# Reordering the first attention step of a delta-rule attention and two-MoE kernel, and moving the router's set-up into the dense rounds

## The chip, the cores and the metric

The kernel runs on one core of a Trainium2 chip. The time is device microseconds of one execution; the median of three runs before the change is 1247.72 us (1247.0 to 1248.55). The core has five instruction streams, each in order: TensorE (PE, with its weight loads PEld), VectorE (DVE), ScalarE (ACT), GpSimd (POOL) and SyncE (SP), which here issues nearly all DMAs. A stream stops at an instruction whose inputs, or whose output buffer, are not ready, and everything behind it in that stream stops too.

## The reference

Three stages, each feeding the next, over 3072 tokens of width 384:

```python
# 1. delta-rule attention, 32 (batch, head) pairs, 768 steps, width 48
for t in range(S):
    y[:, :, t] = einsum('bhd,bhde->bhe', q[:, :, t], state)
    v_old = einsum('bhde,bhd->bhe', state, kt)
    state += beta_t * einsum('bhd,bhe->bhde', kt, vt - v_old)
# 2. dense MoE, 4 experts, hidden width 1024
for e in range(4):
    out += p[:, e:e+1] * (relu(x @ w1[e]) @ w2[e])
# 3. sparse MoE, 8 experts: cosine router with the normalized expert_emb and tau, each token to its best expert
expert_idx = argmax(xn @ en.T / tau, axis=1)
out[mask] = gate_w[mask, None] * (relu(x[mask] @ w1[e]) @ w2[e])
```

## The kernel before, in words

Attention is done in NS = 12 steps of 64 tokens for all 32 pairs at once (two groups x = 0, 1 of eight pair products each). Every value is kept as a sum of two fp16 halves (hi and lo), so each product is three matmuls, and most tiles are made by an ACT instruction for hi and a DVE or POOL instruction for lo. A step loads K, Q, V, normalizes K, transposes K and Q, forms the Gram matrices (`gram_k`, `gram_q`), inverts a triangular matrix on DVE (`inverse`, the "pivots"), solves for W through Z and Y with the right hand side R (`rest`, `solve_z`, `solve_y`, `solve_w`), writes the new state (`state`, `keep_state`) and the outputs xT (`outputs`, `columns`).

The dense MoE works in 16 rounds per step: round i does `hidden(i+1)` (18 matmuls, L569), then the attention pieces of slot 2i, then `second(i)` (12 matmuls, L591), then the pieces of slot 2i+1. ACT makes H hi (L573) and DVE H lo (L574) between the two. Every fourth `second` ends an expert, and its two sums in PSUM are added into the tiles acc0 and acc1: for the first expert by ACT (L599), otherwise by DVE (L601). PSUM holds two such sums, so the next expert's first `second` waits for that.

All order is written by hand: tables of slots (`SLOTS`, `FIRST`, `SECOND`) say when each piece of a step is emitted. The first step (`FIRST`) has nothing to run beside; its slots from -5 to 31 are emitted ahead of the first round. The pieces of step s >= 1 go into the rounds of step s-1.

Beside this the kernel has to prepare things in the same streams:
- The dense weights: 32 halves of 384 KB (`load_w`) are loaded by SP, each split (`split_w`, L552, L556, L557) by two ACT instructions and one of POOL. Twelve are split in the first step and twenty in the rounds (slots 0 to 22).
- The router's set-up: `setup_a` (constants, and the DMAs of expert_emb into the buffer of acc0 and of tau), `setup_b` (casts, a 3-wide index table, norm of expert_emb, split into `eh`; DVE with two trips to ACT), `setup_c` (PE turns `eh`, ACT copies it to `en`; POOL makes an index image in the buffer of acc0 and zeros in the buffer of acc1, and these go out by DMA to `ids` and `xb`).

The last point matters for buffers: acc0 and acc1 have one buffer each (`bufs=1`), and `setup_c` borrows them:

```python
t = ap.tile([128, 384], F32, name="acc0")[0:96, 0:256]
...
z = ap.tile([128, 384], F32, name="acc1")[0:64]
nc.gpsimd.memset(z, 0.0)
...
nc.sync.dma_start(out=rows[:, :, lo:hi], in_=z...)
```

SP issues its DMAs in program order. Eight are in flight: each waits for the DMA eight places earlier. In the first 75 us they are: K, Q, V of step 0 and beta, eight weight halves, K of step 1, fourteen halves, Q of step 1, ten halves, the probabilities p, V of step 1; then the DMA transposes KTB<-KB of step 1 (L207), which wait for K's split into KB (L163, L164).

Of the kernel before, what the change touches and what calls it, by code (L numbers as in the profile page):

```python
# [8 lines left out]
F32 = mybir.dt.float32  # L9
# [22 lines left out]
class Attention:  # L32
# [3 lines left out]
    def __init__(self, ctx, tc, q, k, v, beta, ident, pp, xt_pool):  # L36
# [41 lines left out]
        self.t0 = self.cp.tile([128, 16, 32], F16, name="t0")  # L78
        li = self.li = self.cp.tile([128, 2], I32, name="li")
        nc.gpsimd.iota(li[:, 0:1], pattern=[[0, 1]], base=0, channel_multiplier=1)  # L80
        ti = self.ti = self.wk.tile([128, 16, 32], I32, name="ti", tag="wa")
        nc.gpsimd.iota(ti, pattern=[[-2, 16], [1, 32]], base=0, channel_multiplier=0)
        self.TB = zeroed("TB", [128, 16, 2, 128])
        self.WB = [zeroed(f"WB{x}", [128, 2, 8 * 96 + 32]) for x in range(2)]
        self.SB = [zeroed(f"SB{x}", [128, 2, 8 * 96 + 32]) for x in range(2)]

# [414 lines left out]
class Dense:  # L501
# [114 lines left out]
class Sparse:  # L616
# [648 lines left out]
```

## Time and profile before

| | |
|---|---|
| median of 3 runs | 1247.72 us |
| the profiled execution: its time | 1246.16 us |
| its span in the trace | 1244.4 us |
| PE busy | 1141.7 us (92%) |
| DVE, ACT, POOL busy | 770.1, 627.6, 382.8 us |
| first matmul of the dense rounds (L569) | at 74.07 us |
| first `second` of the rounds (L591) | at 83.75 us |

The span is the time from the first to the last recorded instruction; 1.8 us of the execution lie around it. A row of the timeline gives start, duration, engine, line, operation, output<-input with partitions x elements, and in brackets the idle time of that engine in front of it with what ended it. A buffer that is borrowed has its name by the allocation (acc for the router's scratch). Durations of several instructions (x2, x4) run from the first start to the last end.

### The profile page before, as it was taken

The numbers are of one execution on the slowest core, as the hardware profiler recorded it, in microseconds if no ns is written. First come the engines' busy times: TensorE is split into PE (matmuls) and PEld (weight loads), VectorE is DVE, ScalarE is ACT, GpSimd is POOL, SyncE is SP. The second block draws the span as 40 slices with busy tenths as digits, with TensorE's granted clock in tenths as the row PEclk, the third lists the DMA queues.
The fourth block names the chain that finished last, engine by engine and source line by source line (L and its number), as shares of the span: only waits on it lengthen the run. The fifth ranks groups of instructions, "written<-read, shape, count | busy, mean of one in ns | idle before, by whom it ended". The sixth has DMA issues, their size and how long they took to land. (4 is left out here: it accounts for less than half of the span.)

```text
span 1244.4 us, 34015 instructions
## 1 busy us (share of the span) xinstructions
PE 1141.7 (92%) x13738; PEld 892.0 (72%) x13738; DVE 770.1 (62%) x2811; ACT 627.6 (50%) x1163; POOL 382.8 (31%) x356
## 2 busy tenths in 40 slices
PE   3078899999999999999999999999999999999997
PEld 3066676777777777777777776777777777878886
DVE  7847558777587776877768767687684434212221
ACT  5758655555555555656556565565653142222222
POOL 7637422332323223233233332333321113222221
PEclk9579899999999999999999999999999999999999
DMA  8980144555725555254563555634631094967950
GB/s 177 231 147 17 27 90 120 116 88 138 107 86 108 92 148 104 77 121 79 150 110 93 120 118 136 122 95 115 110 102 29 20 346 96 355 176 242 319 157 29
DMA packets 246162, 159.17 MB, mean 128 GB/s; under 512 B 195231, under 2 KB 229356, under 8 KB 246000
## 3 DMA queue, kind: packets, MB, share of 16 engines
q1 hardware_dynamic: 241600, 147.26, 51.4%
q0 software_dynamic: 4400, 9.68, 2.5%
q8 instruction: 110, 1.80, 0.7%
q14 instruction: 52, 0.43, 0.2%
HBM read 142.53 MB, written 35.80 MB: 143 GB/s over the span
## 5 line engine op out<-in xcount | busy, mean ns | idle before, releaser
L591 PE MATMUL po<-W,H 128*128 128x384 f16 x2304 | 410.9, 328 | 25.0 <-DVE acc L601 11.4
L569 PE MATMUL ph<-xT,W 128*128 128x256 f16 x3456 | 409.8, 274 | 1.5 <-ACT xT L106 1.5
L569 PEld LDWEIGHTS <-W 128*128 128x128 f16 x3456 | 332.1, 98 | 49.2 <-issue 1.8
L591 PEld LDWEIGHTS <-H 128*128 128x128 f16 x2304 | 220.0, 98 | 166.0 <-DVE H L574 16.6
L574 DVE SCALAR_TENSOR_TENSOR H<-ph,H 128x512 f16<-128x512 f32 x192 | 132.0, 688 | 204.1 <-ACT H L573 203.6
L573 ACT ACTIVATE H<-ph 128x512 f16<-128x512 f32 x192 | 113.9, 593 | 143.5 <-PE ph L569 142.0
L755 POOL TENSOR_TENSOR wso<-wst,wso 128x768 f16<-128x768 f32 x64 | 105.7, 1651 | 260.9 <-ACT wst L754 253.0
L1024 DVE SCALAR_TENSOR_TENSOR H<-ph,H 128x512 f16<-128x512 f32 x54 | 37.2, 690 | 154.5 <-ACT H L1023 154.5
L1019 PE MATMUL ph<-xt,slot 128*128 128x128 f16 x1944 | 114.7, 221 | 2.0 <-DMA xt<-g 2.0
L1019 PEld LDWEIGHTS <-slot 128*128 128x128 f16 x1944 | 112.3, 99 | 5.7 <-issue 2.4
L304 DVE TENSOR_TENSOR tt<-tt,pr 128x60 f32<-128x60 f32 (+34 forms) x660 | 111.0, 210 | 0.7
L1036 PE MATMUL po<-slot,H 128*128 128x384 f16 x648 | 110.1, 326 | 0.6 <-DVE H L1024 0.6
L300 DVE TENSOR_TENSOR pr<-tt,KQ 128x60 f32<-128x60 f32 (+34 forms) x660 | 109.0, 203 | 0.8
L1036 PEld LDWEIGHTS <-H 128*128 128x128 f16 x648 | 62.1, 98 | 39.1 <-DVE H L1024 1.0
L1041 POOL DMA_INDIRECT out_dram<-ob,idx x27 | 27.4, 1014 | 170.7 <-ACT ob L1040 80.7
L753 ACT ACTIVATE wso<-wst 128x768 f16<-128x768 f32 x64 | 53.3, 833 | 43.7 <-issue 25.5
L1023 ACT ACTIVATE H<-ph 128x512 f16<-128x512 f32 x54 | 32.2, 597 | 80.2 <-PE ph L1019 77.3
L329 PEld LDWEIGHTS <-TB 128*128 128x128 f16 x1152 | 34.6, 98 | 44.4 <-POOL W L557 24.2
L557 POOL TENSOR_TENSOR W<-W,W 128x768 f16<-128x768 f32 x30 | 50.8, 1705 | 42.8 <-ACT W L556 25.5
L263 POOL TENSOR_TENSOR AO<-G,AO 32x256 f16<-32x256 f32 x48 | 31.7, 660 | 97.9 <-ACT AO L262 95.9
L840 POOL DMA_INDIRECT ids<-idt,si x24 | 25.1, 1045 | 118.8 <-DMA ids<-idt,si 65.4
L1040 ACT ACTIVATE ob<-po,sm 128x384 f32<-128x384 f32 x27 | 15.7, 580 | 82.1 <-PE po L1036 82.0
(253 smaller groups left out, 1447.0 us busy)
## 6 DMA issues: line engine op xcount, KB each, us to landing
slot<-wimg SPq DMA_DIRECT2D x108, 768.0 KB
wst<-in_moe_w_dram SPq DMA_DIRECT2D x65, 384.0 KB
wimg<-wso SPq DMA_DIRECT2D x64, 384.0 KB
W<-in_moe_w_dram SPq DMA_DIRECT2D x15, 384.0 KB
xb<-xr SPq DMA_DIRECT2D x48, 98.0 KB
Kr<-in_k_dram SPq DMA_DIRECT2D x24, 192.0 KB
Qr<-in_q_dram SPq DMA_DIRECT2D x24, 192.0 KB
Vr<-in_v_dram SPq DMA_DIRECT2D x24, 192.0 KB
```

Source lines behind the costliest of these rows:

```text
L300: nc.vector.tensor_tensor(out=p, in0=t[:, :, j:j + 1].to_broadcast([128, m, j]), in1=AT[:, j, 0:j].unsqueeze(1).to_broadcast([128, m, j]), ...
L304: nc.vector.tensor_tensor(out=t, in0=t, in1=p, op=ALU.subtract)
L557: low.tensor_tensor(out=lo, in0=t, in1=hi, op=ALU.subtract)
L569: nc.tensor.matmul(ph[:, i], w1[:, a, k, 128 * i:128 * i + 128], xT[:, b, k], start=(n == 0), stop=(n == 8))
L573: nc.scalar.activation(out=H[:, 0], in_=ph, func=AF.Relu)
L574: nc.vector.scalar_tensor_tensor(out=H[:, 1], in0=ph, scalar=0.0, in1=H[:, 0], op0=ALU.max, op1=ALU.subtract)
L591: nc.tensor.matmul(po[t], H[:, a, i, 128 * t:128 * t + 128], w2[:, b, i], start=(f == 0 and i == 0 and n == 0), stop=(f == 3 and i == 1 an ...
L753: self.nc.scalar.activation(out=o[:, 0], in_=t, func=AF.Copy, scale=scale)
L755: self.nc.gpsimd.tensor_tensor(out=o[:, 1], in0=t, in1=o[:, 0], op=ALU.subtract)
L1019: nc.tensor.matmul(ph[:, i], w[:, a, k, 128 * (i % 2):128 * (i % 2) + 128], xt[:, 3 * b + k], start=(m == 0), stop=(m == 8))
L1024: nc.vector.scalar_tensor_tensor(out=H[:, 1], in0=ph, scalar=0.0, in1=H[:, 0], op0=ALU.max, op1=ALU.subtract)
L1036: nc.tensor.matmul(po, H[:, a, i], w[:, b, i % 2], start=(q == 0 and i == 0 and m == 0), stop=(q == 1 and i == 3 and m == 2))
```

## The change

It concerns the first step, the router's set-up and the splits of the dense weights.
- In `FIRST`: `rest` (R) goes from slots 19, 21 to -1, `gram_q` from 2 to 1, `z`, `y`, `w` from 23, 24, 26 to 20, 22, 24, `out` from 28 to 25 (now ahead of `state` at 27), the K norm of step 1 to slots 8, 20, 25.
- `align` is a DVE copy while `low` is DVE; `low` is POOL from slot 4 to 27, DVE before and behind (K's split for step 1, at slot 28, goes to DVE), and POOL in the rounds.
- The memsets of TB, WB and SB on POOL come behind `setup_a`, which moves ahead of the first step; `setup_columns` moves there too.
- Ten weight halves are split in the first step and 22 in the rounds, slots 0 to 24, each by itself.
- `setup_b` moves from slot 20 of the first step to slot 3 of the rounds, `setup_c` from slot 1 to slot 6.

```diff
+FIRST = dict(SLOTS, split_k=(-5, -5), split_q=-3, turn_k=(-1, -1), turn_q=0, rest=(-1, -1), gram_k=(1, 1),
+             gram_q=(1, 1), align=3, to_lanes=4, split_g=(4, 4), split_p=(4, 4), expand_s=None, init=5,
+             pivots=(1, 3, 3, 2, 3, 2, 3, 2, 3, 2, 3, 3, 1), from_lanes=18, split_t=18, z=20, y=22, w=24, out=25,
+             state=27, keep=27, load_k=2, load_q=18, load_v=22, norm=(8, 20, 25))
...
+    def zero_later(self):
+        for t in self.later:
+            self.nc.gpsimd.memset(t, 0.0)
...
+        if self.low is self.nc.vector:
+            self.nc.vector.tensor_copy(self.G32[r, :, 0:32], self.G32[r, :, 32:64])
+        else:
+            self.nc.scalar.activation(out=self.G32[r, :, 0:32], in_=self.G32[r, :, 32:64], func=AF.Copy)
...
     def setup_b(self, sp, ap):
         nc, cp = self.nc, self.cp
+        sq = ap.tile([128, 384], F32, name="acc1")[0:8]
+        ss = self.ess = cp.tile([8, 1], F32, name="ess")
+        nc.scalar.activation(out=sq, in_=self.em, func=AF.Square, accum_out=ss)
...
-    first[3] += [lambda: sparse.setup_a(sp, dense.ap)]
-    first[5] += [lambda: splits(0, 3)]
-    for n in range(3, 9):
-        first[n + 3].append(lambda n=n: splits(n, n + 1))
     first[19] += [lambda: loads(22, 32), dense.load_p]
-    first[20] += [lambda: splits(9, 11), lambda: sparse.setup_b(sp, dense.ap)]
-    first[22] += [lambda: splits(11, 12)]
+    for n, o in enumerate((5, 5, 5, 6, 7, 8, 9, 20, 22, 24)):
+        first[o].append(lambda n=n: splits(n, n + 1))
     loads(0, 8)
+    sparse.setup_a(sp, dense.ap)
+    attn.zero_later()
+    attn.setup_columns()
...
     for o in range(-5, 32):
-        if o == 4:
-            attn.low = nc.gpsimd
+        attn.low = nc.gpsimd if 4 <= o < 28 else nc.vector
...
-    at[1].append(lambda: sparse.setup_c(sp, dense.ap))
+    at[3].append(lambda: sparse.setup_b(sp, dense.ap))
+    at[6].append(lambda: sparse.setup_c(sp, dense.ap))
```

ACT, rounds 1 and 2 before: between a weight half and H of round 3 stands one attention piece (AO0, hi of the Gram part).

```order
L552 ACTIVATE W1_1_3_175<-W1_2_0_177 128x768 [waits DMAHW6_49,DMAHW5_49,Pool_49]
L556 ACTIVATE W1_2_0_177<-W1_2_0_177 128x768 [waits Activation_49]
L262 ACTIVATE AO0_118<-G32_1080 32x8x32 x2
L573 ACTIVATE H_1243<-ph_1224 128x512 [waits DVE_49,PE_49]
L262 ACTIVATE AO1_120<-G32_1080 32x8x32 x2
```

ACT at the same place now (the lines are those of the changed kernel: L565 and L572 the split, L275 AO, L589 H).

```order
L565 ACTIVATE W1_1_2_168<-W1_1_3_170 128x768 [waits DMAHW3_49,Pool_49]
L572 ACTIVATE W1_1_3_170<-W1_1_3_170 128x768 [waits Activation_49]
L275 ACTIVATE AO0_122<-G32_1044 32x8x32 x2
L694 ACTIVATE acc1_1170,ess_1171<-acc0_202 8x384 [waits DMASW0_49]
L741 ACTIVATE nrm_1187<-ess_1171 8x1 [waits DVE_49]
L622 ACTIVATE eh_1197<-acc0_202 8x384 [waits DVE_49]
L589 ACTIVATE H_1219<-ph_1200 128x512 [waits PE_49]
```

The three ACT instructions of `setup_b`, two of them waiting for DVE, now stand ahead of H.

ACT from that H to the first expert's end, before (PT0 and PT1 are attention pieces, acc0 and acc1 the first expert's sums).

```order
L573 ACTIVATE H_1243<-ph_1224 128x512 [waits DVE_49,PE_49]
L262 ACTIVATE AO1_120<-G32_1080 32x8x32 x2
L552 ACTIVATE W2_1_3_176<-W2_2_0_178 128x768 [waits DMAHW7_49,Pool_49]
L556 ACTIVATE W2_2_0_178<-W2_2_0_178 128x768 [waits Activation_49]
L573 ACTIVATE H_1321<-ph_1302 128x512 [waits DVE_49,PE_49]
L269 ACTIVATE PT0_125<-P32_1265 128x512 [waits DVE_49]
L599 ACTIVATE acc0_1364<-po_1110,p_669 128x384 [waits DMAHW2_49,DMASW2_49,DMAHW4_49,PE_49,Pool_49]
L599 ACTIVATE acc1_1365<-po_1111,p_669 128x384 [waits DMAHW1_49,DMAHW3_49,DMAHW0_49,DMAHW5_49,PE_49,Pool_49]
L269 ACTIVATE PT1_126<-P32_1265 128x512 [waits DVE_49]
```

The same stretch of ACT now (L615 the sums).

```order
L589 ACTIVATE H_1219<-ph_1200 128x512 [waits PE_49]
L275 ACTIVATE AO1_124<-G32_1044 32x8x32 x2
L565 ACTIVATE W2_1_2_169<-W2_1_3_171 128x768 [waits DMAHW4_49,Pool_49]
L572 ACTIVATE W2_1_3_171<-W2_1_3_171 128x768 [waits Activation_49]
L589 ACTIVATE H_1297<-ph_1278 128x512 [waits PE_49]
L282 ACTIVATE PT0_129<-P32_1241 128x512 [waits DVE_49]
L565 ACTIVATE W1_1_3_170<-W1_2_0_172 128x768 [waits DMAHW6_49,DMAHW5_49,Pool_49]
L572 ACTIVATE W1_2_0_172<-W1_2_0_172 128x768 [waits Activation_49]
L720 ACTIVATE en_1350<-ps_1343 128x48 [waits PE_49]
L615 ACTIVATE acc0_1361<-po_1074,p_658 128x384 [waits DMAHW2_49,DMASW2_49,DMAHW4_49,PE_49,Pool_49]
L615 ACTIVATE acc1_1362<-po_1075,p_658 128x384 [waits DMAHW1_49,DMAHW3_49,DMAHW0_49,DMAHW5_49,PE_49,Pool_49]
L282 ACTIVATE PT1_130<-P32_1241 128x512 [waits DVE_49]
```

A weight half and `en` have come in front of the sums. The waits of the sums are the same names as before: DMASW2 is the DMA of the index image out of acc0, DMAHW0 and DMAHW1 are the two of the zeros out of acc1.

POOL, `setup_c` before (L708 to L713), among weight halves (L557) and attention pieces.

```order
L557 TENSOR_TENSOR W2_1_2_174<-W2_1_3_176,W2_1_2_174 128x768 [waits Activation_49]
L708 IOTA ti2_1166 96x256 [waits PE_49]
L709 CAST acc0_1165<-ti2_1166 96x256 [waits Pool_49]
L710 DMA ids_77<-acc0_1165 96x256 [waits Pool_49]
L713 MEMSET acc1_1170 64x384
L557 TENSOR_TENSOR W1_1_3_175<-W1_2_0_177,W1_1_3_175 128x768 [waits DMAHW6_49,DMAHW5_49,Activation_49]
```

POOL, `setup_c` now (L724 to L729).

```order
L573 TENSOR_TENSOR W2_1_2_169<-W2_1_3_171,W2_1_2_169 128x768 [waits Activation_49,Pool_49]
L283 TENSOR_TENSOR PT0_129<-P32_1241,PT0_129 128x512 [waits Activation_49]
L573 TENSOR_TENSOR W1_1_3_170<-W1_2_0_172,W1_1_3_170 128x768 [waits DMAHW6_49,DMAHW5_49,Activation_49]
L724 IOTA ti2_1353 96x256 [waits PE_49]
L725 CAST acc0_1352<-ti2_1353 96x256 [waits Pool_49]
L726 DMA ids_77<-acc0_1352 96x256 [waits Pool_49]
L729 MEMSET acc1_1357 64x384
```

It stands behind the lo part of the weight half W1_1_3, the same half that ACT splits just ahead of `en` and the sums.

## Rows read from the trace of the kernel before

**Rows 1.** The page, span in 40 slices: DMA busy share in tenths

```profile
DMA  8980144555725555254563555634631094967950
```

**Rows 2.** Windows: us, busy time of each engine, granted clock, DMA share, GB/s

```profile
0.00:75.00 75.00, 22.16 (x388) 20.10 (x389) 58.44 (x213) 43.69 (x74) 45.81 (x52) 0.69 1.00 199
140.00:1244.00 1104.00, 1067.00 (x12829) 832.78 (x12827) 669.59 (x2435) 535.79 (x1016) 301.06 (x275) 0.99 0.53 127
```

**Rows 3.** Waits of PE, 80 to 160 us: total us, times, longest

```profile
PE ps L230 <- DVE KQ L222: 3.2, 1, 3.2
PE po L591 <- DVE acc L601: 3.2, 1, 3.2
PE psz L329 <- ACT R L341: 2.1, 1, 2.1
...
PE psz L329 <- DVE R L342: 1.6, 1, 1.6
```

**Rows 4.** Timeline of SP, 65 to 83 us

```profile
65.24 8.26 SPq L517 DMA_DIRECT2D p<-in_moe_domain_probs_dram  x4
73.61 1.31 SPq L120 DMA_DIRECT2D Vr<-in_v_dram  x2
77.79 5.05 SPq L207 DMA_TRANSPOSE KTB<-KB  x2
```

**Rows 5.** Waits of SP's own queue, 0 to 95 us

```profile
SPq L545 <- DMA W<-in_moe_w_dram: 7.5, 7, 1.4
```

**Rows 6.** Timeline, K's split for step 1 and the first Gram product

```profile
75.88 4.07 POOL L164 TENSOR_TENSOR KB<-Kr,KB 64x384 f16<-64x384 f32 x4 [4.16 <-ACT KB L163]
...
82.84 1.07 PE L230 MATMUL ps<-KQ,KTB 128*128 128x64 f16 x24 [3.22 <-DVE KQ L222]
```

**Rows 7.** Timeline, setup_b in the first step, and POOL beside it

```profile
52.12 0.17 DVE L680 CAST em<-ti 128x8 f32<-128x8 int32 x1
...
53.36 3.24 POOL L557 TENSOR_TENSOR W<-W,W 128x768 f16<-128x768 f32 x2 [6.29 <-DMA W<-in_moe_w_dram]
...
54.95 0.15 DVE L731 RECIPROCAL nrr<-nrm 8x1 f32<-8x1 f32 x1 [0.97 <-ACT nrm L725]
55.13 1.47 DVE L732 TENSOR_TENSOR nrr<-nrr,ess 8x1 f32<-8x1 f32 x1
...
57.76 0.52 ACT L606 ACTIVATE eh<-acc 8x384 f16<-8x384 f32 x1 [2.85 <-DVE acc L693]
```

**Rows 8.** Timeline and a window, setup_c: POOL, SP, and the DMA engines behind it

```profile
92.16 0.37 POOL L708 IOTA ti<- 96x256 int32 x1
...
93.84 0.44 POOL L713 MEMSET acc<- 64x384 f32 x1
...
94.31 1.26 SPq L718 DMA_DIRECT2D xb<-acc  x2
...
97.50:98.00 0.50, 0.50 (x7) 0.45 (x5) 0.50 (x2) 0.50 (x1) 0.42 (x2) 1.00 0.36 35
```

**Rows 9.** Timeline of ACT, DVE and PE, rounds 1 to 4

```profile
92.50 0.84 ACT L552 ACTIVATE W<-W 128x768 f16<-128x768 f32 x1
...
94.13 0.84 ACT L262 ACTIVATE AO<-G 32x256 f16<-32x256 f32 x2
...
94.29 1.23 DVE L273 SCALAR_TENSOR_TENSOR KQ<-KQ,bl 128x1024 f32<-128x1024 f32 x1
...
94.99 0.60 ACT L573 ACTIVATE H<-ph 128x512 f16<-128x512 f32 x1
...
99.61 0.62 ACT L269 ACTIVATE PT<-P 128x512 f16<-128x512 f32 x1
...
101.33 1.07 ACT L599 ACTIVATE acc<-po,p 128x384 f32<-128x384 f32 x2 [1.10 <-issue]
...
103.54 2.11 PE L591 MATMUL po<-W,H 128*128 128x384 f16 x12
```

**Rows 10.** Timeline of DVE, the lo part of step 1's right hand side

```profile
135.17 1.74 DVE L342 SCALAR_TENSOR_TENSOR R<-Vr,R 128x384 f16<-128x384 f32 x1 [2.31 <-ACT R L341]
```

More of the change, by code (lines that the diff above doesn't have):

```diff
@@ L23 @@
     load_k=1, load_q=16, load_v=18, norm=(8, 18, 24))
-FIRST = dict(SLOTS, split_k=(-5, -5), split_q=-3, turn_k=(-1, -1), turn_q=0, gram_k=(1, 1), gram_q=(2, 2), align=3, to_lanes=4, split_g=(4, 4),
-             split_p=(4, 4), expand_s=None, init=5, pivots=(1, 3, 3, 2, 3, 2, 3, 2, 3, 2, 3, 3, 1), from_lanes=18, split_t=18,
-             rest=(19, 21), z=23, y=24, w=26, state=27, keep=27, out=28, load_k=2, load_q=18, load_v=22, norm=(18, 18, 21))
+FIRST = dict(SLOTS, split_k=(-5, -5), split_q=-3, turn_k=(-1, -1), turn_q=0, rest=(-1, -1), gram_k=(1, 1),
+             gram_q=(1, 1), align=3, to_lanes=4, split_g=(4, 4), split_p=(4, 4), expand_s=None, init=5,
+             pivots=(1, 3, 3, 2, 3, 2, 3, 2, 3, 2, 3, 3, 1), from_lanes=18, split_t=18, z=20, y=22, w=24, out=25,
+             state=27, keep=27, load_k=2, load_q=18, load_v=22, norm=(8, 20, 25))
 SECOND = dict(SLOTS, split_k=(-5, -5), turn_k=(-4, -4), split_q=-3, turn_q=-2, sum_k=(-1, -1), gram_k=(0, 1), align=2, to_lanes=3, split_g=(3, 4), init=5,
@@ L43, in __init__, with zeroed @@
         self.wk = ctx.enter_context(tc.tile_pool(name="attw", bufs=1))
-        def zeroed(name, shape, eng=nc.gpsimd):
+        self.later = []
+        def zeroed(name, shape, eng=nc.gpsimd, later=False):
             t = cp.tile(shape, F16, name=name)
-            eng.memset(t, 0.0)
+            if later:
+                self.later.append(t)
+            else:
+                eng.memset(t, 0.0)
             return t
@@ L56, in __init__ @@
         self.QT = zeroed("QT", [128, 2, 8, 2, 64], nc.vector)
+        li = self.li = self.cp.tile([128, 2], I32, name="li")
+        nc.gpsimd.iota(li[:, 0:1], pattern=[[0, 1]], base=0, channel_multiplier=1)
+        ti = self.ti = self.wk.tile([128, 16, 32], I32, name="ti", tag="wa")
+        nc.gpsimd.iota(ti, pattern=[[-2, 16], [1, 32]], base=0, channel_multiplier=0)
         make_identity(nc, ident)
@@ L78, in __init__ @@
         self.t0 = self.cp.tile([128, 16, 32], F16, name="t0")
[L79 to L85, printed above, removed]
+        self.TB = zeroed("TB", [128, 16, 2, 128], later=True)
+        self.WB = [zeroed(f"WB{x}", [128, 2, 8 * 96 + 32], later=True) for x in range(2)]
+        self.SB = [zeroed(f"SB{x}", [128, 2, 8 * 96 + 32], later=True) for x in range(2)]
         NS = self.NS
@@ L247, in align @@
         r = slice(64 * h + 32, 64 * h + 64)
-        self.nc.scalar.activation(out=self.G32[r, :, 0:32], in_=self.G32[r, :, 32:64], func=AF.Copy)
+        if self.low is self.nc.vector:
+            self.nc.vector.tensor_copy(self.G32[r, :, 0:32], self.G32[r, :, 32:64])
+        else:
+            self.nc.scalar.activation(out=self.G32[r, :, 0:32], in_=self.G32[r, :, 32:64], func=AF.Copy)
     def to_lanes(self):
@@ L545, in load_w, with split_w @@
             eng.dma_start(out=t[96:128], in_=self.w1[e, 288:384, cols].rearrange("(i r) f -> r i f", r=32))
-    def split_w(self, n, low):
+    def split_w(self, n, low, pool=False):
         nc = self.nc
@@ L555, in split_w @@
         else:
-            nc.scalar.activation(out=t, in_=t, func=AF.Copy, scale=scale)
+            if pool:
+                nc.gpsimd.tensor_scalar(out=t, in0=t, scalar1=scale, scalar2=None, op0=ALU.mult)
+            else:
+                nc.scalar.activation(out=t, in_=t, func=AF.Copy, scale=scale)
             low.tensor_tensor(out=lo, in0=t, in1=hi, op=ALU.subtract)
@@ L636, in setup_a @@
         nc.gpsimd.dma_start(out=t, in_=self.tau.unsqueeze(0).to_broadcast([128, 1]))
-        sq = ap.tile([128, 384], F32, name="acc1")[0:8]
-        ss = self.ess = cp.tile([8, 1], F32, name="ess")
-        nc.scalar.activation(out=sq, in_=em, func=AF.Square, accum_out=ss)
         self.tri = cp.tile([128, 128], F16, name="tri")
@@ L1099 @@
     for o in range(-5, 32):
-        if o == 4:
-            attn.low = nc.gpsimd
+        attn.low = nc.gpsimd if 4 <= o < 28 else nc.vector
         for g in first[o]:
             g()
+    attn.low = nc.gpsimd
     at = defaultdict(list)
@@ L1114 @@
     at[0][:0] = second[-1]
-    for n, o in enumerate((0, 1, 2, 4, 7, 8, 9, 10, 11, 12, 13, 14, 15, 16, 16, 18, 20, 21, 21, 22)):
-        at[o].append(lambda n=n: splits(12 + n, 13 + n))
-    at[1].append(lambda: sparse.setup_c(sp, dense.ap))
+    for n, o in enumerate((0, 1, 2, 4, 6, 8, 9, 10, 11, 12, 13, 14, 15, 16, 17, 18, 19, 20, 21, 22, 23, 24)):
+        at[o].append(lambda n=n: splits(32 - len((0, 1, 2, 4, 6, 8, 9, 10, 11, 12, 13, 14, 15, 16, 17, 18, 19, 20, 21, 22, 23, 24)) + n, 33 - len((0, 1, 2, 4, 6, 8, 9, 10, 11, 12, 13, 14, 15, 16, 17, 18, 19, 20, 21, 22, 23, 24)) + n))
+    at[3].append(lambda: sparse.setup_b(sp, dense.ap))
+    at[6].append(lambda: sparse.setup_c(sp, dense.ap))
     at[2].append(dense.norm_p)
```

1 line of the change is left out of this document (removed).

## The prediction

> **What bounds the kernel now.** I read the page's table of engines and its slices first, then busy time and clock by stage, then the waits of PE where two stages meet, then the timeline of each engine there, and last the order of the instructions before and now.
>
> From 140 us on PE is busy 1067 of 1104 us at a granted clock of 0.99 [rows 2]. No instruction of PE changes, so whatever happens before 140 us reaches the end as a plain shift, and the question is only when PE arrives at 140 us.
>
> Up to 75 us the limit is another one. PE is busy 22 of 75 us, but the DMA engines 1.00 of it, at 199 GB/s [rows 1, 2], and SP's own queue waits seven times, 7.5 us in sum, for weight DMAs eight places back [rows 5]. SP's order ends with p, V of step 1 and the transposes KTB of step 1. Issuing p's pieces spans 65.24 to 73.50, V ends at 73.61 + 1.31 = 74.92, and the transposes go out only at 77.79 [rows 4]. They waited for KB, whose first lo part POOL ends within 75.88 to 79.95 [rows 6]: two limits lie close together there.
>
> Between 80 and 160 us PE stands still for some 10 us in four large pieces [rows 3]: 3.2 ahead of the Gram product, put down to KQ but ending with the transposes KTB (77.79 + 5.05 = 82.84) [rows 4], 3.2 for a sum in acc, 2.1 and 1.6 for R of step 1.
>
> **The first step: -2.8 us.** R goes ahead of the pivots, outputs ahead of the state, `setup_b` leaves from between the two parts of R, and K's split for step 1 goes from POOL to DVE. `setup_b` alone took 52.12 to 57.76 + 0.52 = 58.28, that is 6.16 us [rows 7]; POOL's split of K 4.07 us [rows 6], of which I take half as the gain of the other engine, for want of a row; R's two parts ahead of the pivots some 3 us, an estimate from the 0.6 to 1.7 us that such a part takes on each engine [rows 9, 10]. So the compute chain is some 11 us earlier. But SP's list of DMAs is the same as before, and the DMA engines are full up to there. The transposes can go right behind V, at 74.92 in place of 77.79: 2.87 us. They take 5.05 us, the Gram product follows at once [rows 4, 6]. I take -2.8. The other 8 us become a wait of PE for the transposes. Ends: -1.5 (p's issue, which is bound by landing DMAs, gets slower because more compute runs beside it) and -3.5 (some of the weight DMAs start earlier, since fewer splits stand ahead of their buffers). Should SP not be the limit, all 11 pass: a rival.
>
> What that queue hides, costed at nothing: the memsets of TB, WB, SB later, `setup_columns` earlier, `align` on DVE, the K norm's slots, ten in place of twelve weight halves. What hides them is the 8 us just named; only what exceeds it would show.
>
> **`setup_b` and `setup_c` in the rounds: +10.8 us.** I follow ACT and POOL in the clock of before, from [rows 9]. ACT's order is now: half, AO0, `setup_b`, H, AO1, half, H, PT0, half, en, sums. `setup_b` on DVE starts when DVE is done with KQ: 94.29 + 1.23 = 95.52. Its length was 6.16 us; of that 0.97 us was a trip to ACT where the root stood in ACT's queue, of which I take off 0.75; 5.4 us are left, and `eh` is done at 100.9. Those 5.4 still hold one peculiar wait: L732, an 8x1 product, took 1.47 us where L731 of the same shape took 0.15, and it ended at 56.60, just when POOL's second lo of a weight half ended (53.36 + 3.24) [rows 7]. Without such a wait the length is 4.1; if it came behind everything that POOL has in this window (one half of 1.62 and smaller pieces) it is about 8.4. I take 5.4, since POOL has a half's lo here too.
>
> Beside the row stands a rule. The Trainium skill (SBUF — State Buffer, Who interferes with whom) says that DVE and GpSimd share a port pair under a lock which is held for a whole instruction. By it 1.3 to 4.3 us of `setup_b` would be such waits; the trace agrees as far as L732 ending with POOL's instruction goes.
>
> Then ACT: H 0.60 (101.5), AO1 0.84 (102.35), a half of twice 0.84 (104.05), H 0.60 (104.65), PT0 0.62 (105.3), the half W1_1_3 1.68 (107.0). POOL must first make the lo of this half, 1.62 (half of the 3.24 in [rows 7]): 108.6. Only behind it stands `setup_c`: iota to the end of the memset was 92.16 to 94.28, 2.12 us: 110.7. The zeros go out through SP; before, that DMA was issued at 94.31 and the DMA engines had fallen to 0.36 by 97.50 to 98.00 [rows 8], so 3.6 us for it: 114.3. The sums of the first expert are written to the same two buffers, acc0 and acc1, and ACT's instruction waits for these DMAs. In before the sums came at 101.33, 3.4 us behind the zeros, and did not notice. Now acc1 is written at 114.3 + 0.54 = 114.85 (half of 1.07 for one).
>
> Queued behind the sums on ACT are PT1 and H of the next round. Waiting for the sums is PE: the `second` that begins expert 2 needs their PSUM buffers. Its first three matmuls were at 103.54 and the next at 103.54 + 0.53 = 104.07 (a quarter of 2.11) [rows 9]. 114.85 - 104.07 = 10.8. Ends: 9.6 (`setup_b` 4.1) and 13.8 (`setup_b` 8.4). A part could be given back by the later 3.2 us wait for acc L601 [rows 3], where PE would arrive later; but PE's granted clock was 0.69 over the first 75 us, where it mostly stood [rows 2], so a stand of 11 us may cost clock too; I set the two against each other.
>
> The two halves that are now split in the rounds and not in the first step cost ACT 2 x 1.68 and POOL 2 x 1.62 us, but at slots 17 to 24, where PE always has matmuls and ACT is 61% busy (669.59 of 1104) [rows 2]: nothing. As many halves as before stand ahead of the first expert's end but for the one named.
>
> **R of step 1: -1.6 us.** PE waited 2.1 and 1.6 us for it [rows 3]; two weight halves stood ahead of its hi part on ACT, and its lo part took 1.74 us on DVE [rows 10]. Now one half stands ahead of it: one half less is 1.68 us. Ends: 0 (DVE is the later one anyway) and -2.8 (the lo part too is free of POOL).
>
> **Sum.** -2.8 + 10.8 - 1.6 = +6.4 us on the profiled execution: 1246.16 + 6.4 = 1252.6. The median 1247.72 is 1.56 above that execution; on it, 1254.0. The bounds of the terms: -3.5 + 9.6 - 2.8 = +3.3 and -1.5 + 13.8 + 0 = +12.3; both far ends together are unlikely, so the likeliest case's own range is 1250 to 1258.
>
> **Rivals.**
> - A, the sums don't stand for `setup_c`'s DMAs: the DMA queue is quiet by then (share 0.36), or POOL gets to `setup_c` much earlier. For it: DMA share from 140 us on is only 0.53. Against it: POOL's lo of W1_1_3 stands ahead in its order, and the 3.6 us are a row's. Then only ACT's own delay is left: the sums end at 107.0 + 1.07 = 108.1, 4.1 behind 104.07; -2.8 + 4.1 - 1.6 = -0.3: 1247.4, no change. Chance 0.17.
> - B, SP is not the limit and the whole head of 11 us passes: for it, the transposes waited for KB and not for SP in before; weights could be loaded sooner. Against it, V's issue at 74.92, and a DMA share of 1.00. -11 + 10.8 - 1.6 = -1.8, and down to -8 with rival A besides: 1245.9, about 1240 at the far end. Chance 0.12. It decides from a head gain of about 9 us on.
> - C, the locks pile up: DVE's small instructions of `setup_b` each wait for POOL, and `setup_b` takes 8.4 us. -2.8 + 13.8 - 1.6 = +9.4: 1257. For it, the 1.47 us of L732; against it, that only one of `setup_b`'s instructions showed this beside POOL's work. Chance 0.10.
>
> **How the numbers follow.** The forecast has 0.61: 1254.0. The range goes from B's value to a little above C's: 1246 to 1259, which leaves out B's far end, about half of B, and the tail of C, some 0.15. The measurement can tell 0.2%, 2.5 us, from no change: faster below 1245.2, slower above 1250.2. Faster holds most of B and the lower tail of A (0.11); same holds the rest of A and B (0.18), slower the forecast and C (0.71).
>
> **What would show it.** The transposes KTB go out at about 75 us, right behind V, and PE stands some 8 to 12 us ahead of the Gram product of step 1, behind the first two `hidden`: the first term is right; if the transposes go out at 67, B is. ACT stands 6 to 8 us idle ahead of the first expert's sums with the DMA of xb or ids as the releaser, and PE behind it for some 8 to 11 us: the second term. If ACT has no such idle time, A holds. `setup_b`'s span in the rounds, 5.4 or 8.4, tells C. The waits for R of step 1 come to about 2 us in place of 3.7. PE's busy time beyond 140 us stays; if it changes by over 3 us, the plain shift is wrong, and with it the whole sum.

## The result and the profile after

| | before | after |
|---|---|---|
| median | 1247.60 us (4 runs) | 1258.81 us (4 runs, 1257.5 to 1261.79) |
| ratio, 95% interval | | 1.0092 [1.0072, 1.0113] |
| the profiled execution: time, span | 1246.16, 1244.4 us | 1259.61, 1257.9 us |
| PE, DVE, ACT, POOL busy | 1141.7, 770.1, 627.6, 382.8 | 1144.5, 776.7, 625.4, 379.3 |

Slower, by 11.2 us, where 6.3 were forecast (1254.0); 1258.81 lies at the very edge of the range (1259), the ratio just over it (1259 / 1247.72 = 1.0090).

The waits of PE from 60 to 200 us, after (in all, times, longest):

```profile
PE ps L240 <- DVE KQ L232: 14.6, 1, 14.6
PE po L607 <- ACT acc L615: 5.9, 2, 3.5
PE ps L718 <- DVE P L252: 4.2, 1, 4.2
PE psz L342 <- DVE R L355: 1.6, 1, 1.6
...
PE po L607 <- DVE acc L617: 1.3, 1, 1.3
...
PE psz L342 <- ACT R L354: 0.2, 1, 0.2
```

Set beside [rows 3]: the wait ahead of the Gram product (L240) went from 3.2 to 14.6 us, two new waits came (5.9 for ACT's sums, 4.2 for P), R of step 1 went from 3.7 to 1.8, the sum on DVE from 3.2 to 1.3.

SP's timeline, after, ahead of that Gram product:

```profile
65.02 8.40 SPq L530 DMA_DIRECT2D p<-in_moe_domain_probs_dram  x4
73.53 1.31 SPq L130 DMA_DIRECT2D Vr<-in_v_dram  x2
75.36 5.17 SPq L217 DMA_TRANSPOSE KTB<-KB  x2
```

In place of [rows 4]: the transposes stand right behind V now, 0.5 us after it, and KB waits for SP instead of SP for KB.

PE's timeline, after, from that product to step 1's R (L607 is `second`, L585 `hidden`, L718 `setup_c`'s turn of eh):

```profile
80.89 1.62 PE L240 MATMUL ps<-KQ,KTB 128*128 128x64 f16 x24 [14.57 <-DVE KQ L232]
...
101.76 0.29 PE L718 MATMUL ps<-ident,eh 8*128 8x8 f16 x6 [4.16 <-DVE P L252]
101.98 3.78 PE L607 MATMUL po<-W,H 128*128 128x384 f16 x12
105.59 2.13 PE L585 MATMUL ph<-xT,W 128*128 128x256 f16 x18
111.20 0.65 PE L607 MATMUL po<-W,H 128*128 128x384 f16 x3 [3.48 <-ACT acc L615]
114.25 3.04 PE L607 MATMUL po<-W,H 128*128 128x384 f16 x9 [2.40 <-ACT acc L615]
117.08 3.09 PE L585 MATMUL ph<-xT,W 128*128 128x256 f16 x18
120.00 2.11 PE L607 MATMUL po<-W,H 128*128 128x384 f16 x12
...
133.77 2.15 PE L607 MATMUL po<-W,H 128*128 128x384 f16 x12 [1.25 <-DVE acc L617]
```

The `second` at 101.98 took 3.78 and the `hidden` at 117.08 3.09 us, where undisturbed ones take 2.11 and 2.13: PE's granted clock fell behind its stands. By stretches (columns as in [rows 2]):

```profile
100.00:110.00 10.00, 5.96 (x36) 3.74 (x37) 7.30 (x35) 5.47 (x10) 7.38 (x9) 0.83 0.03 10
110.00:120.00 10.00, 6.40 (x30) 3.79 (x30) 3.88 (x25) 6.83 (x10) 2.64 (x2) 0.66 0.19 41
120.00:130.00 10.00, 10.00 (x96) 7.45 (x94) 7.17 (x47) 9.64 (x15) 7.04 (x6) 1.00 0.01 2
```

What ACT, POOL and SP did meanwhile, after:

```profile
105.39 0.19 ACT L720 ACTIVATE en<-ps 128x48 f16<-128x48 f16 x1
110.57 0.58 ACT L615 ACTIVATE acc<-po,p 128x384 f32<-128x384 f32 x1 [4.99 <-issue]
113.62 0.58 ACT L615 ACTIVATE acc<-po,p 128x384 f32<-128x384 f32 x1 [2.47 <-DMA xb<-acc]
```

```profile
92.30 2.71 POOL L573 TENSOR_TENSOR W<-W,W 128x768 f16<-128x768 f32 x1 [1.87 <-PE ph L585]
...
105.72 1.65 POOL L573 TENSOR_TENSOR W<-W,W 128x768 f16<-128x768 f32 x1
107.32 0.35 POOL L724 IOTA ti<- 96x256 int32 x1
...
108.43 0.56 POOL L726 DMA_DIRECT2D ids<-acc  x1 [0.30 <-POOL acc L725]
108.98 0.44 POOL L729 MEMSET acc<- 64x384 f32 x1
```

```profile
109.45 1.26 SPq L734 DMA_DIRECT2D xb<-acc  x2
```

ACT has nothing to do from 105.6 on and stands 4.99 us for acc0 and 2.47 us for acc1. The second stand ends with the zeros' DMAs, issued at 109.45, at 113.62. The first the trace puts down to "issue", that is, to nothing that it shows; the instruction waits for the index image's DMA too, which POOL issued at 108.43, and in e2 below, where both borrowers have other buffers, both stands are gone. That is the wait that was forecast, instruction by instruction; in [rows 8, 9] the same DMAs did not hold the sums.

How far a kernel lies behind the first trace of before is read here from ACT's H, which follows each `hidden`: its start in a round, less the start in the same round before (at 90.6, 109.6, 194.3 and 1012.4 us there); a minus is ahead. The experiments below are shown in the same way. The column at 90.6 shows the head; what is added up to 109.6 is the router's set-up, and what is added from there to 194.3 holds R; the sparse stage is what follows 1012.4. At 109.6 ACT's H of before ran 2.0 us behind its `hidden`, so H hides a part: PE itself lies 12.55 us behind there in the first trace of the changed kernel (`second` at 120.00 against 107.45), and gets 1.9 of it back at the next sum on DVE.

| kernel | at 90.6 | at 109.6 | at 194.3 | at 1012.4 | sparse stage, us | ratio to before, 95% |
|---|---|---|---|---|---|---|
| before, four traces | 0, -0.8, -3.0, -4.2 | the same | 0, -0.5, -2.9, -4.0 | 0, -1.2, -1.5, -3.8 | 232.1, 230.0, 235.4, 232.2 | |
| changed, three traces | -2.0, -2.0, -3.1 | 10.6, 10.7, 9.7 | 9.4, 9.5, 8.5 | 10.5, 9.5, 13.9 | 235.1, 233.9, 233.6 | 1.0092 [1.0072, 1.0113], 1.0077 [1.0051, 1.0104] |
| e2 own tiles | -3.6 | 3.4 | 2.4 | 3.1 | 234.9 | 1.0037 [1.0020, 1.0055] |
| e3 back | -4.5 | -4.7 | -6.0 | -5.1 | 234.0 | 0.9988 [0.9971, 1.0005] |
| e4 SP's order | -3.6 | 9.4 | 8.1 | 9.1 | 233.6 | 1.0086 [1.0060, 1.0112] |
| e6 late weights | -10.0 | 2.2 | 1.0 | 0.3 | 231.5 | 1.0016 [0.9998, 1.0035] |
| e7 late weights, back | -5.5 | -2.5 | -3.7 | -3.3 | 230.9 | 0.9986 [0.9969, 1.0003] |
| e8 own tiles, tables back | -4.4 | 0.0 | -1.0 | -0.5 | 233.2 | 1.0005 [0.9987, 1.0023] |
| e9 R late | -2.1 | 10.6 | 9.4 | 10.4 | 232.6 | 1.0093 [1.0065, 1.0122] |
| e10 before, set-up moved | -2.5 | 9.6 | 8.5 | 8.7 | 236.0 | 1.0093 [1.0063, 1.0123] |
| e11 late, back, own tiles | -6.2 | -6.2 | -7.2 | -6.4 | 234.3 | 0.9949 [0.9930, 0.9968] |
| e12 late, set-up spread | -10.2 | -10.1 | -3.1 | -1.3 | 232.4 | 0.9987 [0.9970, 1.0005] |
| e16 the same, other slots | -11.1 | -11.1 | -8.1 | -7.4 | 232.9 | 0.9968 [0.9947, 0.9990] |

### The profile page after: what moved, and what is told of

Its sections match the earlier page's. It is cut to its first block, busy times and chain, and to the rows that moved or that the text cites. A ratio compares the mean times of both kernels' runs of the same rounds, so it can differ in the third digit from the quotient of the medians.

```text
span 1257.9 us, 34011 instructions
## 1 busy us (share of the span) xinstructions
PE 1144.5 (91%) x13738; PEld 888.5 (71%) x13738; DVE 776.7 (62%) x2817; ACT 625.4 (50%) x1161; POOL 379.3 (30%) x352
## 5 line engine op out<-in xcount | busy, mean ns | idle before, releaser
L607 PE MATMUL po<-W,H 128*128 128x384 f16 x2304 | 412.7, 328 | 31.2 <-DVE acc L617 9.8
L585 PE MATMUL ph<-xT,W 128*128 128x256 f16 x3456 | 409.5, 273 | 0.3
L585 PEld LDWEIGHTS <-W 128*128 128x128 f16 x3456 | 331.9, 98 | 48.3 <-issue 1.2
L607 PEld LDWEIGHTS <-H 128*128 128x128 f16 x2304 | 220.0, 98 | 174.4 <-issue 22.5
L589 ACT ACTIVATE H<-ph 128x512 f16<-128x512 f32 x192 | 113.8, 593 | 140.3 <-PE ph L585 137.4
L240 PE MATMUL ps<-KQ,KTB 128*128 128x64 f16 x1152 | 42.3, 194 | 15.2 <-DVE KQ L232 15.0
```

The source lines that it names most:

```text
L240: self.nc.tensor.matmul(ps[:, u], self.KTB[x][:, a, u], self.KQ[:, b, 8 * x + u, c:c + 64], start=(j == 0), stop=(j == 2))
L585: nc.tensor.matmul(ph[:, i], w1[:, a, k, 128 * i:128 * i + 128], xT[:, b, k], start=(n == 0), stop=(n == 8))
L589: nc.scalar.activation(out=H[:, 0], in_=ph, func=AF.Relu)
L607: nc.tensor.matmul(po[t], H[:, a, i, 128 * t:128 * t + 128], w2[:, b, i], start=(f == 0 and i == 0 and n == 0), stop=(f == 3 and i == 1 an ...
```

## The experiments

**e1 and e15, the changed kernel again; e5, e13 and e14, the kernel before again.** No edit.

> The changed kernel once more, nothing edited. In its trace PE is 9.0 us behind the kernel before at 200 us, 10.5 us at the end of the dense rounds and 13.5 us at the end of the span. Theory P (the path ahead of 140 us is the whole effect; what came behind 200 us is chance of one execution): shift at 200 us again 8.5 to 9.5 us, but the part behind it changes by some us; median 1256 to 1258. Theory D (a part of the loss arises behind 200 us, because everything runs at another time there): again 1 to 2 us in the dense rounds and about 3 us in the sparse stage; median 1259 to 1261.

> The kernel before once more, nothing edited. All four changed kernels so far lie 0.6 to 1.1 us further behind the first trace of before at the end of the dense rounds than at 200 us, and another 1.6 to 3.0 us at the end of the span (their sparse stage takes 233.6 to 235.1 us, in that trace 232.0). Theory C (chance: that one execution of before was a short one): a second trace of before has a sparse stage of 233.5 to 235 us too, and its span is some 2 us longer. Theory D (the change costs it): again 232.0, and the span 1244 to 1245.

> The kernel before, one more execution's trace. If the last 2 us belong to the change: sparse stage 230 to 232 us again. If to single executions: it lies anywhere from 230 to 236 us, as the thirteen traces so far do.

> The kernel before, a further trace: the same two readings, 230 to 232 us in the sparse stage if the last 2 us belong to the change, anywhere from 230 to 236 us if to single executions.

> The changed kernel, one more execution's trace. If the last 2 us belong to the change: sparse stage 234 to 236 us again, lag at 200 us 9.0 to 9.5. If to single executions: anywhere from 230 to 236 us.

The lag between 90.6 and 194.3 us is the same in all three traces of the changed kernel (it grows by 11.4, 11.5 and 11.5 us), so that part is the program's. The rest scatters from trace to trace: the sparse stage took 230.0 to 235.4 us in before and 233.6 to 235.1 in the changed kernel, and e15 lost another 4 us between 240 and 280 us, alone (e5's 230.0 fits neither of its two theories). What had not been seen is that the head itself differs: before reached 90.6 at 0, -0.8, -3.0 and -4.2 us. The trace that the forecast was made from was the slowest of four. The record names one chip for e13, e14 and e15 and another for e5, so a part of this spread may be the chip's; e13 and e14, on one chip, lie 1.3 us apart. Measured against the mean of the four at 194.3 (-1.9), the changed kernel (mean 9.1) is 11.0 us behind, near the difference of the medians, 11.2; by e1's ratio it is 9.6. At the end of their spans the same seven traces lie 14.8 us apart on average, and whether the 3.8 us behind 194.3 are chance is not settled. The same correction brings the others to within 2.6 us of their ratios (e2: 2.4 + 1.9 = 4.3 us, ratio 4.6; e10: 10.4, ratio 11.6; e11: -5.3, ratio -6.4; e3: -4.1, ratio -1.5 with an interval from -3.6 to +0.6; e16: -6.2, ratio -4.0).

**e10, before with only the set-up moved.**

```diff
-    first[20] += [lambda: splits(9, 11), lambda: sparse.setup_b(sp, dense.ap)]
+    first[20] += [lambda: splits(9, 11)]
...
-    at[1].append(lambda: sparse.setup_c(sp, dense.ap))
+    at[3].append(lambda: sparse.setup_b(sp, dense.ap))
+    at[6].append(lambda: sparse.setup_c(sp, dense.ap))
```

> The kernel before with nothing but setup_b and setup_c moved to slots 3 and 6 of the rounds. The second term of the sum by itself: measured from the head with its place kept to that without, it was 15.3 us at 200 us. One weight half fewer than in the changed kernel stands ahead of the sums (1.7 us), and the first step loses setup_b (hidden behind the transposes but for the 2.9 us by which they waited for KB). Theory P: PE stands for P and for the sums, 10 to 12 us lost there, 2 to 3 gained at the Gram product: 8 to 10 us slower, ratio 1.0065 to 1.008. Rival (the two moves cost so much only together with the changed order): under 5 us, ratio below 1.004.

Measured 1.0093 [1.0063, 1.0123], the middle above the 1.008 expected: these two moves alone cost what the whole change costs. PE's stands in its trace:

```profile
80.53 1.49 PE L230 MATMUL ps<-KQ,KTB 128*128 128x64 f16 x24 [1.84 <-DVE KQ L222]
...
101.20 0.29 PE L702 MATMUL ps<-ident,eh 8*128 8x8 f16 x6 [4.10 <-DVE P L242]
109.02 0.65 PE L591 MATMUL po<-W,H 128*128 128x384 f16 x3 [1.84 <-ACT acc L599]
112.07 3.04 PE L591 MATMUL po<-W,H 128*128 128x384 f16 x9 [2.40 <-ACT acc L599]
```

**e3, the changed kernel with the set-up back.**

```diff
+    first[20] += [lambda: sparse.setup_b(sp, dense.ap)]
...
-    at[3].append(lambda: sparse.setup_b(sp, dense.ap))
-    at[6].append(lambda: sparse.setup_c(sp, dense.ap))
+    at[1].append(lambda: sparse.setup_c(sp, dense.ap))
```

> The changed kernel with setup_b back in slot 20 of the first step and setup_c in slot 1 of the rounds, as before; all else as changed. Theory P: PE reaches the Gram product of step 1 still about 2 us earlier than before, loses nothing at the first expert's end, and keeps the 1.9 us gained at R of step 1: 1247.6 - 4 = 1243.7 (1242 to 1246). Rival (the head's gain hangs on setup_b being gone from it): the Gram product comes when it did before or later, 1246 to 1248. Theory D: 3 to 4 us above 1243.7.

The loss is gone: at 194.3 us it is 15.3 us ahead of the changed kernel and 4.1 ahead of the mean of before. The median shows -1.5 us, which cannot be told from nothing. All other parts of the change together are worth 4 us at most.

**e2, setup_c's scratch in own tiles; e8, besides the tables of setup_b back.**

```diff
-        t = ap.tile([128, 384], F32, name="acc0")[0:96, 0:256]
+        t = cp.tile([96, 256], F32, name="idsrc")
...
-        z = ap.tile([128, 384], F32, name="acc1")[0:64]
+        z = cp.tile([64, 384], F32, name="zsrc")
```

```diff
+    first[20] += [sparse.setup_tables]
...
+    def setup_tables(self):
+        for tf, ti in self.iotas:
+            nc.vector.tensor_copy(tf, ti)
...
     def setup_b(self, sp, ap):
-        for tf, ti in self.iotas:
-            nc.vector.tensor_copy(tf, ti)
```

> The changed kernel with setup_c's index image and zeros in tiles of their own in place of the buffers of acc0 and acc1. Theory P: ACT's sums of the first expert no longer stand for the DMAs of ids and xb; PE's second that begins expert 2 starts at about 107.5 us (its PE predecessor's end) in place of 111.2 and 114.25; the lower clock behind it (2.3 us) goes too; of this some 2 us is lost again at the later sum on DVE. Median 1250 (1248 to 1252). Rival: the sums stand for other things (ACT's weight half, PT0, setup_b), as they do in ACT's order: under 3 us gained, 1256. With theory D besides, some 3 us more than either.

> The changed kernel with setup_c's scratch in tiles of its own, and of setup_b only the norm and split of expert_emb (three ACT trips, some 12 DVE instructions) left in slot 3; the casts and the small index table (4.2 us of DVE) back in the first step. With the own tiles alone PE still lost 6.9 us between the second of round 1 and that of round 3 (4.2 us wait for DVE's P, then 1.7 us of lower clock). Theory V (P stood in DVE's queue behind setup_b's whole length): 4.2 us less, the wait goes and the clock stays up; PE some 4 us earlier at 200 us than with own tiles alone, 1246.5. Theory A (the trips to ACT are the wait): no change, 1250.7.

With own tiles ACT's sums in e2 run without a stop:

```profile
103.84 0.19 ACT L720 ACTIVATE en<-ps 128x48 f16<-128x48 f16 x1
103.93 1.04 ACT L615 ACTIVATE acc<-po,p 128x384 f32<-128x384 f32 x2
```

and PE does not stand there: the lag grows by 7.0 us from 90.6 to 109.6 in place of 12.7. So the borrowed buffers cost 5.7 us of the 12.7; the other 7.0 stay with own tiles. In e8 that is 4.4 us; the wait for P went from 4.16 to 1.58:

```profile
96.85 0.29 PE L721 MATMUL ps<-ident,eh 8*128 8x8 f16 x6 [1.58 <-DVE P L252]
```

So the casts and tables of `setup_b` on DVE are the larger part of that wait, as theory V had it, though 2.6 us went and not 4.2; what is left of `setup_b` has two trips to ACT in it, and products of 8x1 of up to 0.84 us. Not all of the rest is `setup_b`'s. In both, ACT stands for POOL's lo of PT, which is queued behind `setup_c`'s iota, cast and memset, 1.52 us in e2, and in e8:

```profile
105.67 0.84 ACT L144 ACTIVATE ksq<-Kr 128x768 f32<-128x768 f32 x1 [2.33 <-POOL PT L283]
```

That makes the next H late. PE itself loses 6.2 of e2's 7.0 us and 2.2 of e8's 4.4 us ahead of this stand, the rest behind it.

**e4, SP's order; e6, besides six weight halves behind the transposes; e7, that and the set-up back.**

```diff
-             ... load_k=2, load_q=18, load_v=22, norm=(8, 20, 25))
+             ... load_k=2, load_q=18, load_v=30, norm=(8, 20, 25))
...
-    first[2] += [lambda: loads(8, 22)]
-    first[19] += [lambda: loads(22, 32), dense.load_p]
+    first[2] += [dense.load_p, lambda: loads(8, 22)]
+    first[19] += [lambda: loads(22, 32)]
```

```diff
-    first[19] += [lambda: loads(22, 32)]
+    first[19] += [lambda: loads(22, 26)]
+    first[31] += [lambda: loads(26, 32)]
```

> The changed kernel with the DMAs of the probabilities p ahead of the weight halves 8 to 21 (they stood, 8.4 us of SP's time, ahead of the transposes KTB of step 1), and V of step 1 behind the transposes. Theory S (SP's order is what PE's 14.6 us wait ahead of the Gram product is): the transposes go out when KB is ready, at about 68 us in place of 75.4; PE's wait falls to some 8 us, and 6 to 7 us pass to the end: 1252. Rival (bandwidth: the weight DMAs in flight until 71 us share the queues with the transposes): transposes go out early but land at about 78; 2 to 3 us gained, 1256.

> The previous edit (p early, V of step 1 behind the transposes KTB) and besides the last six weight halves (26 to 31) loaded behind the transposes, on the changed kernel. Theory B (what holds the Gram product is the bytes of weights in flight ahead of the transposes, since these went out 6.7 us earlier in the previous run but took 9.0 us in place of 5.2): with 2.3 MB fewer ahead, at 200 to 250 GB/s about 9 us, the transposes go out when KB is ready, at 67 to 68, and take 5 us; PE is some 7 us earlier at the Gram product and at the end than the changed kernel: 1250. Theory S (SP's own issue): no better than the previous run, 1256.

> The same loads as in the run before it, and setup_b and setup_c at their old places. Theory B and P together: no loss at the first expert's end, and the head is bound by the compute chain; with setup_b in the first step that chain is some 5 us longer, KB is ready at about 71: 3 to 4 us better than the run with setup_b and setup_c back alone, about 1240.5 (1238 to 1243). If the DMA order is worth nothing: 1244.

SP's transposes in e4, and in e6:

```profile
68.66 8.98 SPq L217 DMA_TRANSPOSE KTB<-KB  x2
```

```profile
66.75 4.42 SPq L217 DMA_TRANSPOSE KTB<-KB  x2
```

In e4 they go out 6.7 us earlier and take 3.8 us longer, right behind the last weight DMA (issued at 68.10). In e6, with 2.3 MB fewer ahead (last weight DMA at 58.49), they go out as soon as KB is made and take 4.42. PE reaches the Gram product at 71.90 in place of 80.89, and that passes to the end (8.4 us at 194.3). So two limits stand one behind the other. In the changed kernel itself it is SP's list: the DMA engines were all but empty (share 0.08) while SP ended p and issued V, ahead of the transposes:

```profile
73.00:74.00 1.00, 0.00 (x0) 0.00 (x0) 0.00 (x0) 0.00 (x0) 0.00 (x0) 0.50 0.08 2
```

With p out of the way (e4) the transposes meet the weights, and the rival of e4 was right. The Trainium skill (DMA: Bandwidth & Descriptors, Issuing engines are not separate DMA queues) says that DMAs run on the same 16 engines and interleave, whichever engine started them; the 8.98 us against 4.42 agree. The late weights without the new order were not run, so what each is worth alone is known for the order only. e7 gave back 3 us at the first expert's sum:

```profile
100.75 0.58 ACT L615 ACTIVATE acc<-po,p 128x384 f32<-128x384 f32 x1 [3.89 <-DMA xb<-acc]
```

There the zeros' DMAs stood behind the late weights, a third form of the same wait.

**e9, R behind split_t.**

```diff
-FIRST = dict(SLOTS, ..., turn_q=0, rest=(-1, -1),
+FIRST = dict(SLOTS, ..., turn_q=0, rest=(19, 19),
```

> The changed kernel with the right hand side R of step 0 put back behind split_t (slot 19 of the first step) instead of ahead of the pivots. Theory H (the first step's shorter compute chain is hidden behind the transposes KTB, PE waits 14.6 us for them): some 2 to 3 us later at the first hidden, PE's wait shorter by as much, and the Gram product of step 1 where it was (80.9 us, within the 1.5 us by which it differs between executions): same time as the changed kernel, ratio to before 1.008 to 1.009. Rival (the chain passes): 2 to 3 us slower than the changed kernel, ratio 1.010 to 1.011.

The first `hidden` is 1.0 us later (2 to 3 were expected), PE's wait for the transposes 13.1 us in place of 14.6, the Gram product at 80.64, the ratio 1.0093: hidden, as theory H had it, as far as the 1.0 us goes.

**e11, e12 and e16, versions.** e11 is e7 with e2's tiles. e12 and e16 are e6 with own tiles for all of the set-up's scratch and `setup_b` in five pieces:

```diff
+    part = sparse.setup_b(sp, dense.ap)
+    next(part)
+    for o in (19, 21, 23, 25, 27):      # e16: (17, 19, 20, 22, 24)
+        at[o].append(lambda: next(part, None))
+    at[28].append(lambda: sparse.setup_c(sp, dense.ap))      # e16: at[30]
```

> Late weights, p early, V behind the transposes, setup_b and setup_c at their old places, and setup_c's scratch in tiles of its own. In the run without own tiles PE stood 2.65 us for the sum into acc1, since the zeros' DMAs to xb queued behind the six late weight halves. Theory P: that wait goes, 1 us of it is lost at the later sum: 5 to 6 us ahead of before at 200 us, ratio 0.9955 to 0.9965. Rival: PE waits for the sums all the same (ACT's order), 0.9985.

> Late weights, p early, V behind the transposes; expert_emb, its squares, the index image and the zeros in tiles of their own; setup_b cut into five pieces in slots 19 to 27 of the rounds and setup_c in slot 28. Neither stands ahead of the first expert's end, and the first step is free of setup_b. Theory P: PE is 8 to 10 us ahead of before at the Gram product of step 1, loses 1 to 3 us to DVE's small pieces ahead of H in slots 19 to 27: ratio 0.993 to 0.9955. Rival (DVE's pivots of step 1 are the next bound, so that PE meets the sum on DVE with 3 to 5 us more wait): 0.996 to 0.998.

> As e12, with the five pieces of setup_b in slots 17, 19, 20, 22, 24 in place of 19 to 27 and setup_c in slot 30 in place of 28, so that eh is split six slots ahead of the matmuls that need it. If place was the price: PE's wait of 5.2 us for eh goes and most of the 9 us that e12 lost at slots 22 to 30 with it; 8 to 11 us ahead of before at 200 us, ratio 0.991 to 0.9945. If the work itself is: again a loss of 7 to 9 us, ratio 0.998.

e11 is 0.9949, 6.4 us faster than before and by the ratios 16 to 18 faster than the changed kernel; PE has no stand at the sums, only DVE's later one (3.23 us). e12 kept its 10 us to 109.6 and lost 7.0 by 194.3, at a place that neither theory named:

```profile
157.80 0.23 PE L727 MATMUL ps<-ident,eh 8*128 8x8 f16 x3 [5.24 <-ACT eh L622]
```

PE stood for `eh`, whose ACT instruction was queued behind the outputs' copies. In e16 that wait is gone and the loss is 3.0 us. Both missed their ranges: e12 0.993 to 0.9955, and its rival's 0.996 to 0.998; e16 0.991 to 0.9945 if place was the price, and came out between that and the 0.998 of its rival. e16 (0.9968) and e11 can't be told apart by their intervals.

## Why the prediction was wrong, by its own steps

**What bounds the kernel: right.** PE's lag at 140 us stayed to the end, within what single executions add. PE's busy time behind 140 us stayed: 1066.7 us from 150.2 us on, against 1067.0.

**The first step, -2.8 us: this step failed.** Its mechanism stood: the transposes went out behind V, PE's wait grew by 11.4 us, and e9 shows 1.0 us of the head's compute to be hidden. But the size of the gain was read off one execution, as 77.79 - 74.92. In the four traces of before the transposes went out at 77.79, 77.05, 76.53 and 75.26, in the three of the changed kernel at 75.36, 75.07 and 73.86, so the issue was on average 1.9 us earlier (76.66 against 74.76). Of that 1.2 us is left at the Gram product (81.70 against 80.46): the transposes took 0.2 us longer, and PE began some 0.5 us behind them and not at once. At 90.6 it is 0.4, since PE worked more slowly behind its stand. PE in e14, and in e15:

```profile
80.29 1.07 PE L230 MATMUL ps<-KQ,KTB 128*128 128x64 f16 x24 [2.21 <-DVE KQ L222]
81.20 2.12 PE L591 MATMUL po<-W,H 128*128 128x384 f16 x12
```

```profile
79.73 1.63 PE L240 MATMUL ps<-KQ,KTB 128*128 128x64 f16 x24 [13.18 <-DVE KQ L232]
81.17 3.51 PE L607 MATMUL po<-W,H 128*128 128x384 f16 x12
```

Behind a stand of 2.2 us the product took 1.07 and the `second` 2.12; behind 13 to 15 us they took 1.62 and 3.38 to 3.56 in all three traces of the changed kernel, where the granted clock from 76 to 84 us is 0.50, the lower of the two levels (1.2 GHz). The slowest two of before had the longer `second` too (3.80, 3.52), behind stands of 3.22 and 2.99 us, and e10 had the slow product behind one of 1.84. So in the changed kernel the clock fell in every trace and in before in half of them, and the length of the last stand alone does not tell which. By the means the term is -0.4, not -2.8: the stall that was moved in front of PE cost its clock as well. It is the least certain of the three terms: between the two traces that stand first it is -2.0, and on the one chip of e13, e14 and e15 it is +0.5. The bounds given (-1.5 to -3.5) left the clock out, and were reasoned from one trace. The reason stated, SP's list, holds for the changed kernel; e4 and e6 show that the weights stand close behind it.

**`setup_b` and `setup_c`, +10.8 us: right in mechanism, short in size.** From 90.6 to 109.6 us the lag grew by 12.6 to 12.7 us in each of three traces, within 9.6 to 13.8. Two sizes were off. `setup_b` on DVE started at 93.42, in the clock of before (2.0 us later) 95.5 as forecast. By the forecast's measure, to the end of ACT's eh, it took 6.49 us (99.39 + 0.52 - 93.42), not 5.4; with DVE's lo of eh behind it, 7.07:

```profile
93.42 1.61 DVE L696 CAST em<-ti 128x8 f32<-128x8 int32 x1
94.95 0.16 DVE L696 CAST rce<-ti 128x8 f32<-128x8 int32 x1
95.02 0.64 DVE L696 CAST idb<-ti 128x2 f32<-128x2 int32 x1
...
95.79 0.64 DVE L697 COPY e3k<-rce 128x8 f32<-128x8 f32 x1
...
99.39 0.52 ACT L622 ACTIVATE eh<-acc 8x384 f16<-8x384 f32 x1 [1.52 <-DVE acc L709]
99.94 0.55 DVE L623 SCALAR_TENSOR_TENSOR eh<-acc,eh 8x384 f16<-8x384 f32 x1 [0.59 <-ACT eh L622]
100.42 0.69 DVE L590 SCALAR_TENSOR_TENSOR H<-ph,H 128x512 f16<-128x512 f32 x1
101.03 0.68 DVE L252 TENSOR_TENSOR P<-ps,mask 128x512 f32<-128x512 f32 x1
```

The first cast took 1.61 us, ten times the next of its shape, and ended with POOL's lo of a weight half (92.30 + 2.71 = 95.01). By the lock of the Trainium skill (SBUF — State Buffer, Who interferes with whom) such waits were expected; the trace agrees. The forecast kept the one wait of before, 1.47 us at the product L732. Here that product took 0.15, but em, idb and e3k took 1.61, 0.64 and 0.64, each 0.16 or 0.17 before. POOL's instruction itself took 2.71 in place of 1.65; it began 0.02 us behind DVE's KQ of 1.23 us, as the same pair did before (94.29 and 94.31, 2.71 there too). The zeros' DMAs took 4.2 us from the memset to the release in place of 3.6. So PE's second triple began 12.2 us late (10.2 behind the first trace and the head's 2.0), not 10.8. And one stand was not seen at all: DVE's P, queued behind `setup_b`, held PE for 4.16 us a round earlier. It cost nothing of its own in the sum, since PE came to the sums in time for a wait that was there anyway; in e2, without that wait, it is most of the loss. The lower clock was set against the wait for DVE's sum: the clock took 2.4 us (10.2 us of lag at the second triple, 12.6 at the next `second`), the sum gave back 1.9. The two cancelled but for 0.5. In the same step ACT's busy share of 61% is misread: 669.59 is DVE's column, ACT's is 535.79 of 1104 us, 49%; nothing rests on the difference.

**R of step 1, -1.6 us: right.** The lag fell by 1.2 to 1.3 us from 109.6 to 194.3 in each trace; ACT's part of the wait went from 2.14 to 0.22 us, DVE's 1.6 stayed. At R itself PE gained 1.7 to 2.2 us, and 0.9 went again between 163.9 and 168.5 us of before.

**The sum.** -0.4 + 12.7 - 1.3 = 11.0 against -2.8 + 10.8 - 1.6 = 6.4; medians 11.2. (On the median the forecast's sum is 1254.1, not 1254.0.) Of the 4.6 us missing, 2.4 are the head's by the means, 1.9 the set-up's and 0.3 R's. The 1.9 is the same in all three traces; that the rest falls on the head, and that these terms meet the median's 11.2 so closely, is in part luck, given how much single traces scatter.

**The rivals.** A needed sums that don't stand for the DMAs; they stood 7.46 us. B needed the head to pass; the transposes went out at 75.36 and not at 67, which excludes it. C had `setup_b` at 8.4 us; by the same measure it was 6.49, a third of the way from 5.4, and with several short waits, as C had it, in place of one.

## What to carry over

A scratch buffer borrowed from a tile of the main path is free only while its last reader, here a DMA, ends ahead of the owner's next write; moving the borrower later moves that wait onto the owner's engine and onto everything queued there. A gain that is a gap between two queues of one traced execution (3 us here) needs a second trace before it counts: the head of this kernel lay 4 us apart in four traces. Where a stage waits for DMAs, ask for the bytes that stand ahead of the one that is waited for as well as for the issue order: moving the order alone was worth 1 us, moving 2.3 MB of weights that were needed much later another 7.

## What was not expected of the hardware

- Two transposes of KB took 4.4 to 5.5 us in all traces but e4's, and 8.98 us there, right behind the last weight DMAs.
- SP's issue of p took 7.0 to 8.4 us for four DMAs in the traces of the two kernels at the end of the weights' loads, and 6.6 to 7.2 us where it stood early (e4, e6, e7).
- The same program's sparse stage took 230.0 to 235.4 us in four traces. What sets it was not tried.
